# An attention and mixture kernel: the fourth pair's load asked for sooner in the opening, and output by pairs of token blocks on two row tiles with unpadded parts

## The chip, the cores and the metric

The kernel runs on one core of one Trainium2 chip. The metric is the device time of one execution in microseconds (us); lower is better. A core has five engines: TensorE (PE, whose weight loads are listed apart as PEld), VectorE (DVE), ScalarE (ACT), GpSimd (POOL) and SyncE (SP), which in this kernel issues all the DMAs. Each engine works through its own instructions in the order in which the program lists them, and waits on semaphores for the others.

## The reference

Attention over 8 batches and 8 heads, 576 tokens of 64 numbers each, with a decay made of cumulated logarithms of f; then a soft mixture of 8 experts with 4 slots each over all 4,608 tokens. Cut to what matters:

```python
cum = np.cumsum(np.log(np.clip(f, 0.0001, 1.0)), axis=-1)
scores = q @ k.T / 8 + cum[:, None] - cum[None, :]           # causal, per head
attn = softmax(scores) @ v                                    # x: 4608 x 512, heads side by side
logits = x @ phi                                              # 4608 x 32
d = exp(logits - logits.max(0)); d /= d.sum(0) + 1e-09        # over the tokens
slot_input = (d.T @ x).reshape(8, 4, 512)
slot_out[e] = np.maximum(slot_input[e] @ w1[e], 0.0) @ w2[e]  # 512 -> 1024 -> 512
c = exp(logits - logits.max(1)); c /= c.sum(1) + 1e-09        # over the 32 slots
out = c @ slot_out                                            # 4608 x 512
```

The output is 4,608 x 512 numbers of 4 bytes, 9.4 MB. The weights w1 and w2 are 33.6 MB.

## The kernel before, in words

**Attention, by pairs of heads.** There are 32 pairs (`g`, two heads each; head number `i = 2g + h`). `load_qk(g)` brings q and k of a pair, 576 KB, into one of three tiles, `RAW[g % 3]` (line 168). ScalarE rounds them into `WA[g % 3]` and `YA[g % 3]` (`round_k`, `round_q`, lines 177 and 182), DMAs copy the rounded values to the other half of the partitions (`dup_k`, `dup_q`, lines 193 and 197), and GpSimd subtracts them from the raw values, so that `WB` and `YB` hold the low parts (`low_k`, `low_q`, lines 203 and 208). These GpSimd steps are the last readers of a `RAW` tile: a new `load_qk` into it waits for them. TensorE makes the scores once with tokens on the partitions for the row maxima (`s1`, line 224; VectorE takes the maxima in `tops`, line 237; `mturn` and `mrows`, lines 247 to 259, turn them and put them in as a further row of `YA`), and once the other way round for the exponentials (`s2`, lines 274 and 275; `expo` on ScalarE, line 281). GpSimd blanks what lies above the diagonal (`causal`, lines 289 and 292), `s3` (line 309) multiplies by v, `norm` (lines 324 to 329) divides, and `px` (line 336) turns the result. The `s2` products go to a ring of three PSUM banks (`turn`), which `expo` frees; the `s1` products to three others, which `tops` frees.

**The opening.** Lines 496 to 647 are an order written out by hand for the first two pairs, before the loop over `g` from 1 on (line 681). In it SP issues, in this order: the loads of pairs 0 and 1 and the constants, the copies for pair 0, `load_qk(2)` and `load_v(0)` (lines 550 and 551), `dup_k(1)`, `dup_q(1)`, `load_cum(2)` (598 to 600), the row of maxima of head 2 (617), `load_v(1)` and two small constants (618 to 620), `load_qk(3)` (621), the next row of maxima, and the copies for pair 2. `RAW[0]` is the target of `load_qk(3)`; its last reader in the opening is `low_q` of head 1. GpSimd's order there is: `low_k`, `low_q` of heads 0 and 1 (552 to 554), `causal(0)`, `low_k(2)`, `low_q(2)` (608 to 610), `causal(1)`, `low_k(3)`, `low_q(3)` (628 to 630). `first(i, n, busy)` makes the part `n` of the maxima of head `i`, with `busy` matmuls of no use between the scores and the maxima (`warm`, line 489), which keep TensorE at work; `both(i, n)` makes a bank of scores and its exponentials.

**The mixture.** 23 quarters of the weights (512 KB each) have tiles of their own and are loaded during the attention; the other 41 follow into tiles that fall free (`wstream`, line 122). After the last pair come the last logits, the sums over tokens (`dispatch`, line 453), the first layers (`mlp1`, 874; `relu`; `own`, 894) and the second layers (`mlp2`, line 911). `STEPS` sets their order; for experts 4 to 7 the second half of the output's columns is left for the end, lines 997 to 1010.

**The combine weights.** `ctok` holds c for each token; `split(b)` (lines 659 and 660) makes high and low parts of batches b and b + 4 on GpSimd, and `cols(b, ...)` (line 668) turns them, so that `cT` holds, for each token of the first four batches, 128 rows: high and low part of c for a token of the first half (rows 0 to 63) and for the token 2,304 places later (rows 64 to 127).

**The output.** `gathered(n)` (967) sums a half of the 512 columns of the slots' result, `slots(n)` (970) spreads it over the partitions, `halve(h, n)` (976 and 977) makes high and low parts of it for the tokens' half `h`: `SO[h][r]` has values in 64 rows and zeros, set by GpSimd on line 952, in the other 64. `blocks(n0, n1, c)` makes output blocks of 128 tokens: two matmuls over all 128 rows for each (line 992), a copy by ScalarE or VectorE in turn (993) into staging, and one DMA for two blocks (995). The first `FIRST` = 20 blocks of 36 are made in two halves of columns, the others in full width. The staging is six tiles of 1,024 columns, used in turn.

Of the kernel before, what the change touches and what calls it, by code (L numbers as in the profile page):

```python
# [7 lines left out]
F32 = mybir.dt.float32  # L8
# [23 lines left out]
DEFER = 4  # L32
FIRST = 20

# [36 lines left out]
def attn_softmoe(ctx: ExitStack, tc: tile.TileContext, qk, v, f, phi, w1, w2, cst, out):  # L71
# [89 lines left out]
    def turn():  # L161
        ring.append(ring.pop(0))
        return ring[-1]
# [409 lines left out]
    def first(i, n, busy=0):  # L573
        s1(i, *GROUPS[n])
        warm(busy, cs)
        tops(i, *GROUPS[n])
# [6 lines left out]
    for n in range(4):  # L583
        first(0, n, WARM[1])
    first(1, 0, 2 * WARM[1])
    next(r0)
    warm(3 * WARM[1], cs)
    next(r0)
    round_q(1, 0)
    first(1, 1)  # L590
    first(1, 2)
# [4 lines left out]
    round_k(1, 1)  # L596
    round_q(1, 1)
    dup_k(1)
    dup_q(1)
# [20 lines left out]
    nc.sync.dma_start(mk, cst[:, 706:714])  # L620
    load_qk(3)
    round_q(2)
# [31 lines left out]

    def split(b):

        CW[b] = tp.tile([P, NBLK, 2, 2, NS], F32R, name=f"cw{b}", tag="cw", bufs=2)
        hi, lo = (CW[b][:, :, :, r].rearrange("p t h s -> p h t s") for r in range(2))
        nc.gpsimd.tensor_copy(hi, ctok[:, b::4])
        nc.gpsimd.tensor_tensor(lo, ctok[:, b::4], hi.bitcast(F32), op=ALU.subtract)  # L660

# [19 lines left out]
    for g in range(1, NG):  # L681
# [105 lines left out]
        if g == 31:  # L787
            wstream(PTS[:, 0:QW])
            split(0)
            split(1)  # L790
        s3(h1)
# [13 lines left out]
    ring += [ps_s.tile([P, 512], F32, name=f"more{n}", tag="s") for n in range(2)]  # L805
    norm(NH - 1)
    dispatch(b - 1, 0, 1, 2)
    xt(NG - 1, (0, 4), nc.scalar.copy)
# [26 lines left out]
    nc.vector.tensor_scalar_mul(fin[:, 0:2], ones, lrun)  # L835
    split(2)
    dispatch(b, *range(NBLK))
# [81 lines left out]
    for e, k in STEPS[:-4]:  # L919
# [14 lines left out]
        if (e, k) == (3, 0):  # L934
            combine(b, 1)
            combine(b, 2)
            split(3)
        if (e, k) == (0, 6):
            for _ in cols(3, turn):
                pass  # L940
# [18 lines left out]
    pr = [t[:, 0:256] for t in bank]  # L959
    outv = out.rearrange("(n p) c -> p n c", p=P)  # L960
# [10 lines left out]

    def halve(h, *ns):
        rows = slice(64 * h, 64 * h + 64)
        for n in ns:
            c = half[n]
            nc.scalar.copy(SO[h][0][rows, c], pr[n][rows])
            nc.vector.tensor_tensor(SO[h][1][rows, c], pr[n][rows], SO[h][0][rows, c].bitcast(F32), op=ALU.subtract)

    state = [0, 0, 0]

    def blocks(n0, n1, c=slice(0, DM)):

        w = c.stop - c.start
        if state[1] + w * (n1 - n0) > QW:
            state[0:2] = state[0] + 1, 0
        o = stage[state[0] % len(stage)][:, state[1] : state[1] + w * (n1 - n0)]
        state[1] += w * (n1 - n0)
        for n in range(n0, n1):
            h, m = divmod(n, NT // 2)
            pm = turn()[:, 0:w]  # L990
            for r in range(2):
                nc.tensor.matmul(pm, cT[:, 128 * m : 128 * m + 128], SO[h][r][:, c], start=(r == 0), stop=(r == 1))  # L992
            copies[state[2] % 2](o[:, w * (n - n0) : w * (n - n0 + 1)], pm)
            state[2] += 1
        nc.sync.dma_start(outv[:, n0:n1, c], o.rearrange("p (n c) -> p n c", c=w))

# [3 lines left out]
    mlp2(4, 1, 1)  # L1000
    halve(0, 0)
    mlp2(5, 1, 0)
    n = 0
    for e, k in ((5, 1), (6, 0), (6, 1), (7, 0), (7, 1)):
        blocks(n, n + 2, half[0])
        mlp2(e, 1, k)
        blocks(n + 2, n + 3, half[0])
        n += 3
        if n == 9:
            halve(1, 0)  # L1010
    gathered(1)
    blocks(n, n + 2, half[0])
    slots(1)
    blocks(n + 2, n + 3, half[0])
    halve(0, 1)
    blocks(n + 3, FIRST, half[0])
    for n in range(0, FIRST, 2):
        blocks(n, n + 2, half[1])
        if n == 4:
            halve(1, 1)  # L1020
    for n in range(FIRST, NT, 2):
        blocks(n, n + 2)

# [40 lines left out]
```

## Time and profile before

| | |
|---|---|
| time, median of 3 runs | 405.67 us (404.69 to 407.14) |
| the profiled execution's own time | 407.26 us |
| its span, first to last instruction | 405.5 us |
| mean granted TensorE clock | 0.986 |
| busy PE / PEld | 385.3 / 339.3 us |
| busy DVE / ACT / POOL | 281.7 / 259.2 / 257.6 us |
| DMA | 93.72 MB, mean 231 GB/s |

The profile is of one execution, in us from the start of the span. A row of the timeline has the start, the busy time of the rows that were merged, the engine, the line, the operation, the tile written and the tiles read, the shape and the count; in brackets stands how long the engine had been idle before it, and what ended that. A row of a view by windows has, after the window and its length, the busy time of each engine in it with the number of its instructions, the granted clock of TensorE (1.00 is full speed), the mean busy share of the 16 DMA engines, and GB/s.

### The profile page before, as it was taken

The numbers are of one execution on the slowest core, as the hardware profiler recorded it, in microseconds if no ns is written. First come the engines' busy times: TensorE is split into PE (matmuls) and PEld (weight loads), VectorE is DVE, ScalarE is ACT, GpSimd is POOL, SyncE is SP. The second block draws the span as 40 slices with busy tenths as digits, with TensorE's granted clock in tenths as the row PEclk, the third lists the DMA queues.
The fourth block names the chain that finished last, engine by engine and source line by source line (L and its number), as shares of the span: only waits on it lengthen the run. The fifth ranks groups of instructions, "written<-read, shape, count | busy, mean of one in ns | idle before, by whom it ended". The sixth has DMA issues, their size and how long they took to land.

```text
span 405.5 us, 15191 instructions
## 1 busy us (share of the span) xinstructions
PE 385.3 (95%) x5871; PEld 339.3 (84%) x5871; DVE 281.7 (69%) x1127; ACT 259.2 (64%) x660; POOL 257.6 (64%) x351
## 2 busy tenths in 40 slices
PE   7888999999999999999999999999999999899990
PEld 6678999999999999998999999999999885345780
DVE  7784787878787977796879787878787533312571
ACT  8847776767786777686767786778685443100561
POOL 4694788777777777787778777877787742120000
PEclk9996999999999999999999999999999999999997
DMA  6773566677867787768767767777765699999698
GB/s 207 183 183 108 150 174 181 204 205 210 254 192 221 207 238 211 203 191 254 200 197 210 221 205 206 205 207 206 203 172 152 227 360 375 381 408 391 239 368 335
DMA packets 35192, 93.72 MB, mean 231 GB/s; under 512 B 4282, under 2 KB 10096, under 8 KB 35120
## 3 DMA queue, kind: packets, MB, share of 16 engines
q1 hardware_dynamic: 35120, 92.75, 74.0%
q8 instruction: 46, 0.75, 0.8%
q14 instruction: 26, 0.21, 0.1%
HBM read 63.93 MB, written 9.73 MB: 182 GB/s over the span
## 4 chain that ended last, share of the span: by engine, by line
PE 81%; DMA 4%; DVE 3%; ACT 3%; issue 1%; POOL 0%; SPq 0%; DVEq 0%; ACTq 0%
PE pv L309 24%; PE ring L274 13%; PE ring L275 11%; PE s L224 11%; PE pv L336 4%; DMA RAW<-in_qk 3%; PE lg L372 2%; PE pv L911 2%; PE ds L453 2%; PE ring L874 2%; PE pv L874 2%; PE more L992 2%; DVE s L237 1%; DMA out<-RAW 1%; PE ring L911 1%; PE ring L992 1%
## 5 line engine op out<-in xcount | busy, mean ns | idle before, releaser
L281 ACT ACTIVATE PTS<-ring 128x320 f32<-128x320 f32 (+2 forms) x256 | 119.7, 513 | 64.3 <-PE ring L275 36.7
L237 DVE CUSTOM_DVE_ANT_0 s<-s,mask 128x320 f32<-128x320 f32 (+4 forms) x320 | 137.7, 449 | 10.4 <-PE s L224 5.9
L274 PE MATMUL ring<-YA,WA 67*128 67x320 f32 (+9 forms) x384 | 123.3, 334 | 2.7 <-ACT PTS L281 1.7
L275 PE MATMUL ring<-YB,WB 128*128 128x320 f32 (+4 forms) x384 | 111.7, 299 | 0.0
L309 PE MATMUL pv<-V,PTS 128*64 128x65 f32 x3200 | 105.0, 224 | 0.6 <-ACT mr L256 0.6
L309 PEld LDWEIGHTS pv<-V,PTS 128*64 128x64 f32 x3200 | 100.3, 138 | 3.2 <-issue 1.2
L224 PE MATMUL s<-WA,YA 66*128 66x288 f32 (+9 forms) x384 | 98.9, 314 | 1.6 <-ACT YA L182 0.8
L203 POOL TENSOR_TENSOR WB<-RAW,WB 64x576 fp32r<-64x576 f32 x64 | 90.3, 1411 | 11.7 <-DMA WB<-WA 4.9
L208 POOL TENSOR_TENSOR YB<-RAW,YA 64x576 fp32r<-64x576 f32 x64 | 89.3, 1413 | 2.4
L274 PEld LDWEIGHTS ring<-YA,WA 67*128 67x128 f32 (+3 forms) x384 | 70.6, 185 | 9.0 <-issue 2.1
L275 PEld LDWEIGHTS ring<-YB,WB 128*128 128x128 f32 (+1 forms) x384 | 70.8, 184 | 0.0
L224 PEld LDWEIGHTS s<-WA,YA 66*128 66x128 f32 (+1 forms) x384 | 63.6, 192 | 7.3 <-ACT YA L182 1.1
L289 POOL TENSOR_SCALAR_AFFINE_SELECT PTS<-PTS 128x384 f32<-128x384 f32 x64 | 33.3, 521 | 32.0 <-ACT PTS L281 27.8
L292 POOL TENSOR_SCALAR_AFFINE_SELECT PTS<-PTS 128x128 f32<-128x128 f32 (+1 forms) x128 | 31.3, 265 | 34.8 <-ACT PTS L281 32.1
L237 DVE DVE_READ_ACCUMULATOR2_ANT MT<- 128x1 f32 x372 | 52.7, 142 | 0.0
L177 ACT CAST WA<-RAW 64x576 fp32r<-64x576 f32 x64 | 40.0, 669 | 14.2 <-DMA RAW<-in_qk 13.2
L336 PE MATMUL pv<-cs,X 128*128 128x128 f32 x155 | 42.9, 278 | 1.0 <-DVE X L329 0.8
L182 ACT CAST YA<-RAW 64x576 fp32r<-64x576 f32 x64 | 40.0, 670 | 0.4
L237 DVE CUSTOM_DVE_ANT_0 s<-s,mask,MT 128x288 f32<-128x288 f32 x62 | 32.6, 526 | 9.8 <-PE s L224 0.9
L324 DVE TENSOR_SCALAR rl<-pv 128x5 f32<-128x5 f32 x64 | 10.5, 164 | 34.7 <-PE pv L309 33.8
L329 DVE TENSOR_TENSOR X<-pv,rl 128x320 f32<-128x320 f32 (+1 forms) x65 | 31.5, 486 | 2.4 <-DMA YA<-mr 0.3
L360 ACT COPY XT<-pv 128x128 f32<-128x128 f32 (+1 forms) x124 | 28.7, 292 | 0.0
(202 smaller groups left out, 355.1 us busy)
## 6 DMA issues: line engine op xcount, KB each, us to landing
w<-in_w SPq DMA_DIRECT2D x46, 512.0 KB
RAW<-in_qk SPq DMA_DIRECT2D x31, 576.0 KB
V<-in_v SPq DMA_DIRECT2D x32, 325.0 KB
WB<-WA SPq DMA_DIRECT2D x31, 288.0 KB
YB<-YA SPq DMA_DIRECT2D x31, 288.0 KB
p<-in_w SPq DMA_DIRECT2D x7, 512.0 KB
out<-RAW SPq DMA_DIRECT2D x5, 512.0 KB
out<-RAW SPq DMA_DIRECT2D x9, 256.0 KB
```

What stands on the lines that cost most here:

```text
L177: nc.scalar.copy(WA[g % 3][0:64, S * h : S * h + S], RAW[g % 3][64:128, h])
L182: nc.scalar.copy(YA[g % 3][0:64, h, 64:640], RAW[g % 3][0:64, h])
L203: nc.gpsimd.tensor_tensor(t[0:64], RAW[g % 3][64:128, h], t[64:128].bitcast(F32), op=ALU.subtract)
L208: nc.gpsimd.tensor_tensor(YB[g % 2][64:128, h], RAW[g % 3][0:64, h], YA[g % 3][0:64, h, 64:640].bitcast(F32), op=ALU.subtract)
L224: nc.tensor.matmul(t[:, o : o + w], ya[0:m, h, 128 * blk : 128 * blk + 128], wa[0:m, j0 : j0 + w], start=True, stop=True)
L237: nc.vector.tensor_tensor_reduce(out=t[:, o : o + w], in0=t[:, o : o + w], in1=mask[:, m0 : m0 + w], scale=1.0, scalar=top if n == 3 else ...
L274: nc.tensor.matmul(o, wa[0:m, j0 : j0 + n], ya[0:m, h, 64 + i0 : 64 + i0 + w], start=True, stop=False)
L275: nc.tensor.matmul(o, wb[:, j0 : j0 + n], yb[:, h, i0 : i0 + w], start=False, stop=True)
L281: nc.scalar.activation(PT[i % 2][:, SEG_O[bank] : SEG_O[bank] + at], t[:, 0:at], AF.Exp, scale=0.125)
L289: nc.gpsimd.affine_select(d3, d3, pattern=[[0, 3], [1, 128]], compare_op=ALU.is_ge, fill=0.0, base=0, channel_multiplier=-1)
L309: nc.tensor.matmul(o[64 * u : 64 * u + 64, t, :], PT[i % 2][:, at : at + 64], V[:, g % 2, c, 65 * h : 65 * h + 65], start=(c == 0), stop=( ...
L336: nc.tensor.transpose(pm[:, 0:128], x[:, t, 128 * (p % 2) : 128 * (p % 2) + 128], ident)
```

## The change

It has these parts:

1. In the opening, `load_qk(3)` moves from behind `mrows(1, 0, 1)`, `load_v(1)` and two small loads to a place ahead of `dup_k(1)`.
2. In the opening, the second part of the maxima of head 1 is made before the row of maxima of head 0 is turned, with one `warm` matmul after each of the two parts instead of two after the first; two `warm` matmuls instead of three follow.
3. `split` runs on ScalarE (high part) and VectorE (low part) instead of GpSimd; for b = 0 and 1 the two parts are called at different places. `cols(3)` is made after step (1, 6) instead of after step (0, 6).
4. The output is made by pairs: block `m` of the first half of the tokens and block `m` of the second. `SO[r]` has values in all 128 rows; the first block's matmuls read rows 0 to 63, the second's rows 64 to 127, into two PSUM banks. ScalarE copies the one, VectorE the other. The GpSimd zeros go. `FIRST` counts pairs now: the first 8 pairs (16 blocks) are made in two halves of columns. The last `mlp2` calls are no longer interleaved one by one with the blocks, and two PSUM banks join the ring when they fall free.

```diff
-FIRST = 20
+FIRST = 8
...
-    first(1, 0, 2 * WARM[1])
+    first(1, 0, WARM[1])
+    first(1, 1, WARM[1])
     next(r0)
-    warm(3 * WARM[1], cs)
+    warm(2 * WARM[1], cs)
     next(r0)
     round_q(1, 0)
-    first(1, 1)
     first(1, 2)
...
     round_k(1, 1)
     round_q(1, 1)
+    load_qk(3)
     dup_k(1)
     dup_q(1)
...
-    load_qk(3)
     round_q(2)
...
-    def split(b):
+    def split(b, *parts):
...
-        nc.gpsimd.tensor_copy(hi, ctok[:, b::4])
-        nc.gpsimd.tensor_tensor(lo, ctok[:, b::4], hi.bitcast(F32), op=ALU.subtract)
+        if 0 in parts:
+            nc.scalar.copy(hi, ctok[:, b::4])
+        if 1 in parts:
+            nc.vector.tensor_tensor(lo, ctok[:, b::4], hi.bitcast(F32), op=ALU.subtract)
...
-            split(0)
-            split(1)
+            split(0, 0)
+            split(1, 0)
...
     norm(NH - 1)
+    split(0, 1)
+    split(1, 1)
...
-    split(2)
+    split(2, 0, 1)
...
-            split(3)
-        if (e, k) == (0, 6):
+            split(3, 0, 1)
+        if (e, k) == (1, 6):
             for _ in cols(3, turn):
                 pass
...
-            SO = [[sp.tile([P, DM], F32R, name=f"SO{h}{r}") for r in range(2)] for h in range(2)]
-            for h in range(2):
-                for r in range(2):
-                    nc.gpsimd.memset(SO[h][r][64 * (1 - h) : 64 * (1 - h) + 64].bitcast(F32), 0.0)
+            SO = [sp.tile([P, DM], F32R, name=f"SO{r}") for r in range(2)]
...
+    outv = out.rearrange("(h m p) c -> p h m c", h=2, p=P)
...
+    def halve(n):
+        nc.scalar.copy(SO[0][:, half[n]], pr[n])
+        nc.vector.tensor_tensor(SO[1][:, half[n]], pr[n], SO[0][:, half[n]].bitcast(F32), op=ALU.subtract)
...
+        for m in range(m0, m1):
+            pm = [turn()[:, 0:w] for _ in range(2)]
             for r in range(2):
-                nc.tensor.matmul(pm, cT[:, 128 * m : 128 * m + 128], SO[h][r][:, c], start=(r == 0), stop=(r == 1))
-            copies[state[2] % 2](o[:, w * (n - n0) : w * (n - n0 + 1)], pm)
-            state[2] += 1
-        nc.sync.dma_start(outv[:, n0:n1, c], o.rearrange("p (n c) -> p n c", c=w))
+                for h in range(2):
+                    rows = slice(64 * h, 64 * h + 64)
+                    nc.tensor.matmul(pm[h], cT[rows, 128 * m : 128 * m + 128], SO[r][rows, c], start=(r == 0), stop=(r == 1))
+            for h in range(2):
+                copies[h](o[:, h, m - m0], pm[h])
+        if m1 - m0 == 1:
+            nc.sync.dma_start(outv[:, :, m0, c], o[:, :, 0])
+        else:
+            for h in range(2):
+                nc.sync.dma_start(outv[:, h, m0:m1, c], o[:, h])
...
-    halve(0, 0)
-    mlp2(5, 1, 0)
...
+    halve(0)
+    mlp2(5, 1)
+    ring += [bank[0], po[0]]
+    blocks(0, 1, half[0])
+    blocks(1, 2, half[0])
+    mlp2(6, 1)
+    blocks(2, 3, half[0])
+    blocks(3, 4, half[0])
+    mlp2(7, 1)
     gathered(1)
-    blocks(n, n + 2, half[0])
+    blocks(4, 6, half[0])
     slots(1)
...
+    blocks(6, FIRST, half[0])
+    halve(1)
+    ring += [bank[1], po[1]]
+    for m in range(0, FIRST, 2):
+        blocks(m, m + 2, half[1])
+    for m in range(FIRST, NT // 2):
+        blocks(m, m + 1)
```

More of the change, by code (lines that the diff above doesn't have):

```diff
@@ L653, in attn_softmoe @@
     CW = {}
-    def split(b):
-        CW[b] = tp.tile([P, NBLK, 2, 2, NS], F32R, name=f"cw{b}", tag="cw", bufs=2)
+    def split(b, *parts):
+        if 0 in parts:
+            CW[b] = tp.tile([P, NBLK, 2, 2, NS], F32R, name=f"cw{b}", tag="cw", bufs=2)
         hi, lo = (CW[b][:, :, :, r].rearrange("p t h s -> p h t s") for r in range(2))
-        nc.gpsimd.tensor_copy(hi, ctok[:, b::4])
-        nc.gpsimd.tensor_tensor(lo, ctok[:, b::4], hi.bitcast(F32), op=ALU.subtract)
+        if 0 in parts:
+            nc.scalar.copy(hi, ctok[:, b::4])
+        if 1 in parts:
+            nc.vector.tensor_tensor(lo, ctok[:, b::4], hi.bitcast(F32), op=ALU.subtract)
     def cols(b, bank):
@@ L959, in attn_softmoe @@
     pr = [t[:, 0:256] for t in bank]
-    outv = out.rearrange("(n p) c -> p n c", p=P)
     NT = B * S // P
+    outv = out.rearrange("(h m p) c -> p h m c", h=2, p=P)
     stage = [t.rearrange("p a b -> p (a b)") for t in RAW] + p2 + p0
@@ L970, in slots, with blocks @@
         nc.tensor.matmul(pr[n], srep, so[:, half[n]], start=True, stop=True)
[L972 to L977, printed above, removed]
+    def halve(n):
+        nc.scalar.copy(SO[0][:, half[n]], pr[n])
+        nc.vector.tensor_tensor(SO[1][:, half[n]], pr[n], SO[0][:, half[n]].bitcast(F32), op=ALU.subtract)
     state = [0, 0, 0]
-    def blocks(n0, n1, c=slice(0, DM)):
+    def blocks(m0, m1, c=slice(0, DM)):
         w = c.stop - c.start
-        if state[1] + w * (n1 - n0) > QW:
+        n = 2 * w * (m1 - m0)
+        if state[1] + n > QW:
             state[0:2] = state[0] + 1, 0
[L986 to L990, printed above, removed]
-            for r in range(2):
-                nc.tensor.matmul(pm, cT[:, 128 * m : 128 * m + 128], SO[h][r][:, c], start=(r == 0), stop=(r == 1))
-            copies[state[2] % 2](o[:, w * (n - n0) : w * (n - n0 + 1)], pm)
-            state[2] += 1
-        nc.sync.dma_start(outv[:, n0:n1, c], o.rearrange("p (n c) -> p n c", c=w))
+        o = stage[state[0] % len(stage)][:, state[1] : state[1] + n].rearrange("p (h m c) -> p h m c", h=2, c=w)
+        state[1] += n
+        for m in range(m0, m1):
+            pm = [turn()[:, 0:w] for _ in range(2)]
+            for r in range(2):
+                for h in range(2):
[8 more added lines that the diff above has]
+                nc.sync.dma_start(outv[:, h, m0:m1, c], o[:, h])
     gathered(0)
@@ L1000, in attn_softmoe @@
     mlp2(4, 1, 1)
-    halve(0, 0)
-    mlp2(5, 1, 0)
-    n = 0
-    for e, k in ((5, 1), (6, 0), (6, 1), (7, 0), (7, 1)):
-        blocks(n, n + 2, half[0])
[L1006 to L1010, printed above, removed]
+    halve(0)
[7 more added lines that the diff above has]
+    mlp2(7, 1)
     gathered(1)
-    blocks(n, n + 2, half[0])
+    blocks(4, 6, half[0])
     slots(1)
[L1014 to L1022, printed above, removed]
+    blocks(6, FIRST, half[0])
[5 more added lines that the diff above has]
+        blocks(m, m + 1)
 def kernel(q, k, v, f, moe_phi, moe_w1, moe_w2):
```

## The prediction

> **What bounds the kernel now.** I read the page first, then the chain of waits, then windows and the timeline of the two stages that the change touches: the opening, and the output.
>
> ```profile
> span 405.5 us, 15191 instructions
> ...
> PEclk9996999999999999999999999999999999999997
> ...
> RAW<-in_qk SPq DMA_DIRECT2D x31, 576.0 KB
> ```
>
> TensorE has full clock in every slice but the fourth (30 to 40 us) and the last, when its work is done. So the fourth is looked at first: by windows the second pair (g = 1) and the third, and two single microseconds of the second.
>
> ```profile
> 26.98:41.79 14.81, 12.36 (x144) 11.32 (x143) 8.69 (x35) 9.49 (x21) 8.85 (x12) 0.77 0.53 138
> 41.79:50.67 8.88, 8.88 (x145) 8.49 (x143) 7.25 (x30) 6.76 (x17) 6.91 (x11) 1.00 0.49 143
> 30.00:31.00 1.00, 0.11 (x1) 0.00 (x0) 0.97 (x6) 0.98 (x3) 0.00 (x0) 1.00 0.85 205
> 33.00:34.00 1.00, 1.00 (x6) 0.81 (x4) 0.94 (x4) 0.60 (x1) 0.13 (x2) 0.50 0.08 32
> ```
>
> The same 144 matmuls take 14.81 us in one pair and 8.88 in the next, where TensorE never idles: 5.93 us too many. They are idle time (0.11 us busy in the first of the two microseconds) and half clock thereafter (0.50 in the second). Picked rows of the timeline, with the others between them left out, say why TensorE idles.
>
> ```profile
> 13.86 1.42 POOL L208 TENSOR_TENSOR YB<-RAW,YA 64x576 fp32r<-64x576 f32 x1
> ...
> 17.09 0.48 SPq L193 DMA_DIRECT2D WB<-WA  x1
> 20.38 1.41 POOL L203 TENSOR_TENSOR WB<-RAW,WB 64x576 fp32r<-64x576 f32 x1 [1.57 <-PE ring L275]
> 23.56 0.37 SPq L168 DMA_DIRECT2D RAW<-in_qk  x1
> 23.82 0.49 POOL L292 TENSOR_SCALAR_AFFINE_SELECT PTS<-PTS 128x128 f32<-128x128 f32 x2
> 24.61 0.92 PE L309 MATMUL pv<-V,PTS 128*64 128x65 f32 x24 [0.26 <-ACT mr L256]
> 28.78 1.24 ACT L177 CAST WA<-RAW 64x576 fp32r<-64x576 f32 x2 [4.22 <-DMA RAW<-in_qk]
> 29.01 0.33 PE L336 MATMUL pv<-cs,X 128*128 128x128 f32 x1 [0.78 <-DVE X L329]
> 31.78 0.39 PE L274 MATMUL ring<-YA,WA 67*128 67x256 f32 x1 [1.67 <-ACT PTS L281]
> ```
>
> The fourth pair's load is issued at 23.56 and ScalarE stands 4.22 us until it has landed. Its four casts then lie ahead of the exponentials that free the PSUM ring, and TensorE stands 1.67 us at 31.78. The gap of 0.78 us before it is VectorE's (the first `norm`s), and isn't the load's. `RAW[0]`, the target, had its last reader done at 13.86 + 1.42 = 15.28: the load could have gone 8.3 us sooner.
>
> In the last stage the weights stream first, then the output. Here are four rows of its timeline, the first a stall of TensorE before `cols(3)`, and its windows.
>
> ```profile
> 352.52 0.44 PE L668 MATMUL lg<-cs,cw 128*128 128x128 f32 x2 [1.36 <-POOL cw L660]
> ...
> 374.83 3.84 SPq L995 DMA_DIRECT2D out<-RAW  x6
> 381.48 0.59 PE L970 MATMUL ring<-so,cs 128*128 128x256 f32 x2
> 383.15 0.38 PE L992 MATMUL ring<-SO,cT 128*128 128x256 f32 x1 [0.23 <-DVE SO L977]
> ```
>
> ```profile
> 350.00:355.00 5.00, 3.64 (x33) 1.23 (x29) 0.92 (x4) 0.86 (x3) 1.56 (x3) 1.00 1.03 413
> 375.00:380.00 5.00, 4.93 (x46) 3.06 (x44) 2.46 (x6) 2.59 (x7) 0.00 (x0) 1.00 0.74 256
> 380.00:385.00 5.00, 4.77 (x40) 4.00 (x38) 3.37 (x9) 2.63 (x9) 0.00 (x0) 1.00 0.62 212
> 385.00:390.00 5.00, 4.98 (x33) 4.32 (x32) 3.73 (x10) 3.44 (x9) 0.00 (x0) 1.00 1.02 342
> 395.00:400.00 5.00, 1.32 (x6) 0.75 (x4) 1.58 (x3) 1.17 (x2) 0.00 (x0) 1.00 1.05 399
> ```
>
> From 385 on the DMA engines are full (share 1.02 and more) and TensorE ends long before them: the end is output bandwidth. From 375 to 385 they are not (0.74, 0.62), while TensorE is nearly full: there TensorE, with blocks and `mlp2` interleaved, feeds them too slowly, and the second half of the columns can't begin before `slots(1)` at 381.48 and its `halve` at 383.15.
>
> **The change part by part.** The sum is made against the profiled execution: 407.26 us, its span of 405.5 and 1.76 around it. That is 1.59 above the median of 405.67.
>
> *The load.* In its new place SP comes to it behind `load_v(0)` and waits until 15.28; `dup_k(1)`, behind it on SP, is held by ScalarE until 17.09 anyway, so SP's queue loses nothing. The DMA queue may.
>
> ```profile
> 16.00:16.50 0.50, 0.50 (x7) 0.50 (x5) 0.47 (x5) 0.47 (x3) 0.00 (x0) 1.00 1.03 406
> 17.50:18.00 0.50, 0.50 (x4) 0.30 (x2) 0.43 (x2) 0.50 (x2) 0.00 (x0) 1.00 0.00 0
> ```
>
> 576 KB (590,000 bytes) at 406 GB/s are 1.45 us. The engines are full before 17.5, then empty for half a microsecond; the load would move from about 17.4 to 18.9, ahead of `dup_k(1)`. Of the 1.45 us the hole takes about half, so that `dup_k(1)` lands about 0.9 us later (bounds 0 and 1.45). GpSimd's 1.57 us of idleness before 20.38 is the wait for that copy (the matmul named had no part in it), and behind it stand `low_q(2)`, `causal(1)` (ending 23.82 + 0.49 = 24.31) and then `s3(1)` on TensorE at 24.61. That has 0.3 us of slack. So the early load costs TensorE about 0.7 us at 24.61 (0 to 1.15), and VectorE's `norm` behind it as much.
>
> What it gains: the casts run right after the row of maxima at about 24.6 to 27, the exponentials of the second pair no longer wait, and the gap of 1.67 us goes. Late next is VectorE's gap of 0.78, which stays. Half clock began less than a microsecond after the gap; I take it to be the gap's effect, since it is the only one of that size before the output's end: the 1.36 us at 352.52 had no such effect (clock 1.00 in that window).
>
> Without both, pair g = 1 takes what its neighbour takes: 5.93 - 0.78 (gap that stays) - 0.7 (late start) = 4.45 us gained; I take 4.3, since VectorE comes out of its crowded stretch a little behind. Bounds: 5.15 without any delay of `dup_k`; 1.67 - 0.7 = 0.97 if the half clock stays. Behind this stage TensorE is full until the weights' stream, so what is gained here is passed on whole.
>
> The Trainium skill (TensorE: Matmul & The Clock Gate, Part 1) puts the fall to half clock down to an idle window of about 3.4 us, and asks for gaps under some 3 us. Going by that, a gap of 1.67 us would not have done it, and the half clock would have another cause; the trace, with its fall right behind this gap, speaks for a shorter measure.
>
> *The reordered `warm` matmuls.* One is left out, and the second maxima move into a time in which VectorE idles 1.31 us:
>
> ```profile
> 14.39 0.47 DVE L237 CUSTOM_DVE_ANT_0 s<-s,mask 128x288 f32<-128x288 f32 x1 [1.31 <-PE s L224]
> ```
>
> What follows hangs on ScalarE, whose first exponentials start when the first scores are there, at best one `warm` matmul sooner. That is a few tenths, inside the bounds left open above, and nothing if the added score matmul takes its place; it stays out of the sum.
>
> *`split`.* GpSimd's two steps before `cols(3)` become a ScalarE cast and a VectorE subtraction, and `cols(3)` moves behind more `mlp2` work: the 1.36 us at 352.52 go. That is no gain at the end by itself, since the weights' stream fills the DMA there (1.03), but TensorE comes to the last `mlp2` 1.36 us sooner. The parts for b = 0 and 1 cost VectorE about 2 x 0.49 us (as its 128x320 product), ahead of a copy before which it idles 1.37 us; without that cover they would push the last logits back by 1.0.
>
> ```profile
> 28.46 0.49 DVE L329 TENSOR_TENSOR X<-pv,rl 128x320 f32<-128x320 f32 x1
> 334.20 0.42 DVE L345 COPY XT<-ring 128x256 f32<-128x256 f32 x1 [1.37 <-PE ring L336]
> ```
>
> *The output.* The DMA's shortage from 375 to 385 is 5 x (342 - 256) + 5 x (342 - 212) = 1,080 KB, at 342 GB/s 3.2 us. Further, 16 blocks instead of 20 go out in pieces of 1 KB: four blocks, 1.05 MB, at 399 instead of 342, 0.44 us. Ceiling: 3.6.
>
> ```profile
> 374.53 0.43 PE more L992 x2
> 374.96 0.23 PE lg L992 x2
> ```
>
> ```profile
> L993 DVE COPY p<-more 128x256 f32<-128x256 f32 x5 | 2.1, 424 | 0.9 <-PE more L992 0.7
> L993 DVE COPY RAW<-more 128x512 f32<-128x512 f32 x3 | 2.1, 692 | 1.0 <-PE more L992 1.0
> L992 PE MATMUL more<-SO,cT 128*128 128x512 f32 x16 | 4.4, 395 | 0.0
> ```
>
> A block costs TensorE 0.23 us, and 0.20 more behind an `mlp2`; a pair on two row tiles 0.23 if they run beside each other, 0.46 if not; its two copies 0.42, side by side; its 256 KB of DMA 0.77. So either way the DMA is the slowest, once the order lets blocks through. Before `slots(1)` stood 17 blocks (3.9 us of TensorE), and now stand six pairs (1.4 us overlapped, 2.8 not), with TensorE 1.36 sooner: from 381.48 it comes to 377.6 to 379.0. I take 378, and the second half's blocks 1.7 behind it as before (383.15 - 381.48), at 379.7 instead of 383.15. In the meantime eight pairs (2.1 MB) are there for 375 to 380, which can take 1.7. What is left is a gap or two of half a microsecond, where the next DMA waits for a copy. I take 2.3 of the 3.6; bounds 0.5 (blocks late for another reason) and 3.6.
>
> Sum: 407.26 - 4.3 - 2.3 = 400.7.
>
> **The rivals.** *The half clock stays* (its cause is not the gap): 407.26 - 0.97 - 2.3 = 404.0, within half a per cent of the median, about what a measurement can tell from no change. Against it: nowhere else in 400 us does the clock fall while there is work.
>
> *The early load costs what it brings.* Before, 28.78 - 23.56 = 5.2 us went by from its issue to its landing. If it holds `dup_k(1)` till 22.8 instead of 20.38, `s3(1)` starts 2.2 us later, a gap as long as the one removed, with its half clock; the second pair's start is lost about as much as the gap brings, within 0.5: 407.26 + 0.5 - 2.3 = 405.5. It decides from a delay of about 2 us on. Against it: 406 GB/s just before.
>
> *The row tiles don't overlap, nor hide their loads* (slower). Then each matmul costs what a lone one does, 0.38 us at 256 columns and 0.395 at 512. From 379.7 on there are 8 pairs x 4 x 0.38 and 10 pairs x 4 x 0.395, 28.0 us, to 407.7, then the last copy, 0.69, and the last DMA, 4.47 by the chain's row:
>
> ```profile
> 392.14 4.47 DMA out<-RAW
> ```
>
> That is 412.9 against 405.5, 7.4 later; with the opening's 4.3, 407.26 + 7.4 - 4.3 = 410.4. It decides from where a pair costs more than its 0.77 us of DMA, 0.19 a matmul. Against it: 0.115 a matmul now, two in 0.23.
> The Trainium skill (TensorEngine Tiling (Array Packing), Key Properties) says that a change of the tiling mode, though not of the tile alone, drains TensorE, and that tiles take in and multiply in parallel; so it is for this rival only where blocks and `mlp2` alternate, which the change does less often. The 0.20 us more behind an `mlp2` agrees with a drain at a change of mode; no row of before shows two row tiles.
>
> **How the numbers follow.** The forecast has 0.76, the half clock 0.09, the costly load 0.08, the row tiles 0.07. The predicted time is 400.7. The low end is both upper bounds, 407.26 - 5.15 - 3.6 = 398.5; the high end takes in the half clock's 404.0 with a little less from the output, 404.4; outside lie the last two cases and a little of the first. Faster by over half a per cent (below 403.6) is the first case, 0.76; within it the next two, 0.17; slower the last, 0.07.
>
> **What would show it.** Right: the load issued about 15.3, no wait of ScalarE for it, clock 1.00 from 30 to 40 us, the third pair starting about 37.5 instead of 41.79; `low_k(2)` on GpSimd about 21.3; no wait before `cols(3)`; the DMA share near 1 from 376 on (in the new time some 4 us sooner), pairs at 0.23. Wrong: clock 0.50 behind another gap; GpSimd's idle time before 20.38 grown by over 2 us; TensorE full until the last output DMA.

## The result, and the profile after

| | before | after |
|---|---|---|
| median of 20 runs each, side by side | 406.67 us (403.45 to 410.59) | 401.93 us (399.99 to 438.54) |
| the profiled execution: time, span | 407.26, 405.5 us | 404.26, 402.5 us |
| its mean granted clock | 0.986 | 0.971 |

The ratio is 0.989, with a 95% interval of 0.986 to 0.991. The median lies in the forecast's range, 398.5 to 404.4 us, and 1.2 above its point of 400.7. The gain is further off: the sum takes 6.6 us from an execution of 407.26 us, and the medians differ by 4.7. The profile shows why: the half clock, whose removal was half of the forecast's gain (3.3 us: 4.3 with it, 0.97 without), is still there. Two lines of the page after:

```profile
span 402.5 us, 15135 instructions
...
PEclk9959999999999999999999999999999999999985
```

The weak slice was the fourth (30 to 40 us), and is now the third (20 to 30). The windows of after show it at its edges. The third pair starts at 40.17 us in its timeline, where 41.79 was before and 37.5 was forecast. Columns as in the prediction: busy time of PE, PEld, DVE, ACT and POOL, then the clock, DMA share and GB/s.

```profile
17.24:20.65 3.41, 2.01 (x14) 1.53 (x12) 2.66 (x11) 3.36 (x8) 0.49 (x2) 1.00 0.99 295
20.65:24.06 3.41, 3.41 (x34) 3.19 (x35) 2.29 (x12) 2.45 (x6) 2.71 (x2) 0.50 0.45 112
24.06:27.48 3.42, 3.27 (x42) 2.80 (x40) 0.92 (x6) 0.64 (x2) 3.20 (x6) 0.50 0.18 55
27.48:30.89 3.41, 3.41 (x51) 3.06 (x48) 2.06 (x10) 2.10 (x4) 3.40 (x3) 0.50 0.50 97
30.89:34.30 3.41, 3.41 (x31) 3.04 (x27) 3.12 (x15) 1.64 (x5) 0.52 (x1) 1.00 0.96 266
```

Three windows of 3.41 us are at half clock, one more than before (32.64 to 39.47), and they follow one in which TensorE was idle 3.41 - 2.01 = 1.40 us. Each costs up to half its length, 1.7 us. The timeline of after says what that idle time was, and that the load did what was expected of it:

```profile
15.46 0.33 SPq L168 DMA_DIRECT2D RAW<-in_qk  x1
...
18.93 0.47 PE L274 MATMUL ring<-YA,WA 98*128 98x448 f32 x1 [1.40 <-ACT YA L568]
...
21.29 1.40 POOL L203 TENSOR_TENSOR WB<-RAW,WB 64x576 fp32r<-64x576 f32 x1 [2.62 <-DMA WB<-WA]
...
27.09 1.24 ACT L177 CAST WA<-RAW 64x576 fp32r<-64x576 f32 x2
```

The load is issued at 15.46 (15.3 forecast), ScalarE's casts no longer wait for it, and GpSimd's `low_k(2)` starts at 21.29 (21.3 forecast) instead of 20.38. But at 17.5 to 18.9 TensorE waits for a row of maxima (line 568, `next(r1)`). Before had this wait too, shorter, and the prediction doesn't mention it:

```profile
19.06 0.47 PE L274 MATMUL ring<-YA,WA 98*128 98x448 f32 x1 [1.05 <-ACT YA L568]
```

Executions of one kernel differ, among other things, by how many such windows they get; the ratios leave out the few that were much disturbed (the medians and ranges hold all), and where single executions are named, the mean clock of each tells them apart: one window at half clock in 402 us takes 3.41 x 0.5 / 402 = 0.004 from it.

In the output stage the timeline of after has these rows:

```profile
352.10 0.44 PE L671 MATMUL lg<-cs,cw 128*128 128x128 f32 x2
...
371.52 0.38 PE L993 MATMUL ring<-SO,cT 64*128 64x256 f32 x1
371.52 0.38 PE L993 MATMUL more<-SO,cT 64*128 64x256 f32 x1
371.75 0.27 PE L993 MATMUL ring<-SO,cT 64*128 64x256 f32 x1
...
373.72 0.64 PE L916 MATMUL pv<-w,X 128*32 128x256 f32 x8 [0.89 <-DMA w<-in_w]
...
376.25 0.64 PE L916 MATMUL pv<-w,X 128*32 128x256 f32 x8 [0.63 <-DMA w<-in_w]
...
377.47 0.70 PE L972 MATMUL ring<-so,cs 128*128 128x256 f32 x2
...
379.61 0.38 PE L993 MATMUL pv<-SO,cT 64*128 64x256 f32 x1 [0.78 <-ACT SO L975]
```

`cols(3)` no longer waits. The two row tiles start together (371.52 both), and both their second matmuls follow 0.23 us later. `slots(1)` stands at 377.47 (378 forecast, 381.48 before), the second half's first block at 379.61 (379.7 forecast). What wasn't forecast is that TensorE, with less to do, now waits for the weights of the last `mlp2` steps, 0.89 and 0.63 us. The windows of after:

```profile
375.00:380.00 5.00, 3.59 (x38) 1.83 (x36) 2.95 (x8) 2.04 (x7) 0.00 (x0) 1.00 0.64 218
380.00:385.00 5.00, 4.93 (x54) 4.75 (x55) 4.06 (x12) 3.98 (x11) 0.00 (x0) 1.00 1.00 350
```

The DMA is full from 380 on, five microseconds sooner than before (212 GB/s in that window then, 350 now). From 375 to 380 it still isn't (0.64), where I had expected it near 1 from 376.

### The profile page after: what moved, and what is told of

Read it like the earlier page. It is cut to its first block, busy times and chain, and to the rows that moved or that the text cites. A ratio compares the mean times of both kernels' runs of the same rounds, so it can differ in the third digit from the quotient of the medians.

```text
span 402.5 us, 15135 instructions
## 1 busy us (share of the span) xinstructions
PE 379.9 (94%) x5861; PEld 333.7 (83%) x5861; DVE 281.3 (70%) x1127; ACT 258.6 (64%) x660; POOL 251.0 (62%) x339
## 4 chain that ended last, share of the span: by engine, by line
PE 81%; DMA 8%; ACT 2%; DVE 1%; issue 1%; ACTq 0%; DVEq 0%; SPq 0%
PE pv L309 25%; PE ring L274 14%; PE ring L275 12%; PE s L224 12%; DMA w<-in_w 5%; PE pv L336 4%; PE lg L372 3%; PE ds L453 2%; PE pv L879 1%; DMA out<-p 1%; PE pv L916 1%; DMA YA<-mr 1%; DMA out<-RAW 1%; PE pv L247 1%; PE ring L879 1%; PE tk L436 1%
## 5 line engine op out<-in xcount | busy, mean ns | idle before, releaser
L309 PE MATMUL pv<-V,PTS 128*64 128x65 f32 x3200 | 106.9, 226 | 0.5 <-ACT mr L256 0.3
L309 PEld LDWEIGHTS pv<-V,PTS 128*64 128x64 f32 x3200 | 102.1, 140 | 3.4 <-issue 1.4
```

The lines of the kernel that those rows point to most:

```text
L309: nc.tensor.matmul(o[64 * u : 64 * u + 64, t, :], PT[i % 2][:, at : at + 64], V[:, g % 2, c, 65 * h : 65 * h + 65], start=(c == 0), stop=( ...
```

## The experiments

**One part at a time.** Three kernels have one part of the change each; a fourth fills, in the kernel before, the gap of 1.67 us with TensorE work of no use.

The load alone:

```diff
+    load_qk(3)
     dup_k(1)
...
-    load_qk(3)
     round_q(2)
```

> The kernel before with nothing changed but the place of the fourth pair's load, ahead of the second pair's copies. Gap theory (half clock comes when TensorE idles more than about 1.4 us within one window of 3.4 us, and each such window costs TensorE about half of it): the gap of 1.67 us at 30 to 32 us goes, the one at 18 us stays at about 1.0, which did not bring the clock down before; clock 1.00 all through the opening in most executions, second pair (from its first score matmul to the third pair's) about 9.3 instead of 14.8 us, time 3.0 to 4.5 us shorter than before. Stall theory (the half clock belongs to the opening and only its place is accidental): half clock stays somewhere before 45 us, and the time is 1 us shorter. Either way the copy of the second pair lands 0.9 us later, so that GpSimd starts on it at about 21.3 instead of 20.4.

Measured: 403.68 us, ratio 0.993 (0.989 to 0.996). Seven of its 12 executions have clocks of 0.990 to 0.995 (401.82 to 404.78 us); none of the 35 of before that ran beside it is above 0.989 (of the 46 of before that ran beside the later kernels, eight are at 0.990 to 0.992). In the execution that was profiled, `low_k(2)` starts at 21.57, TensorE has no gap above 0.78 us between 20 and 33, the clock is full there from 22.79 on, and the third pair starts at 38.12. So the gap at 31 us and its half clock did go. There is one window at half clock, and it is at another place:

```profile
15.96:19.37 3.41, 2.27 (x18) 1.80 (x17) 3.08 (x14) 3.31 (x8) 1.22 (x6) 1.00 0.98 350
19.37:22.79 3.42, 3.42 (x17) 3.23 (x15) 1.84 (x9) 3.13 (x8) 1.22 (x1) 0.50 0.58 130
```

It follows the old gap of 1.05 us at 18, which in before's profile had no such effect.

The reordered `warm` matmuls alone:

```diff
-    first(1, 0, 2 * WARM[1])
+    first(1, 0, WARM[1])
+    first(1, 1, WARM[1])
     next(r0)
-    warm(3 * WARM[1], cs)
+    warm(2 * WARM[1], cs)
     next(r0)
     round_q(1, 0)
-    first(1, 1)
```

> The kernel before with nothing changed but the order of the second head's maxima and the useless matmuls in the opening (one left out, the second maxima ahead of the turning of the first row). Gap theory: TensorE runs ahead by 0.4 us and then waits for the same ScalarE copy, so the gap at 18 us grows from 1.0 to 1.4 us, half clock comes at about 20 us in a good part of the executions and the gap at 30 us brings it as well in others; time 0 to 2 us longer than before, clock lower. If the reordering is the small gain it looks like on the timeline (ScalarE's chain 0.15 us sooner): 0.1 to 0.2 us shorter, not to be told from the kernel before.

Measured: 404.44 us, ratio 0.996 (0.992 to 0.999). No execution was longer than before's median by more than 0.2 us, and the gain of 2.2 us by medians is more than the 0.1 to 0.2 of the other theory, so both expectations failed. Its timeline shows what this part does to the two gaps of TensorE:

```profile
18.93 0.47 PE L274 MATMUL ring<-YA,WA 98*128 98x448 f32 x1 [1.40 <-ACT YA L568]
...
32.44 0.58 PE L274 MATMUL ring<-YA,WA 67*128 67x256 f32 x1 [2.47 <-ACT PTS L281]
```

The gap at 18 us is 1.40, as in after. In the three other kernels of this group, which have the old order, it is 1.05 or 1.06. So it is the reorder that lengthens it: the second maxima's matmuls used to lie behind the copy of the first row and now lie ahead of it, and TensorE comes to the second row's wait that much sooner. And yet no half clock follows here; the windows give a likely reason:

```profile
17.82:21.24 3.42, 2.31 (x16) 2.05 (x16) 2.79 (x12) 3.35 (x9) 1.48 (x3) 1.00 0.90 182
21.24:24.65 3.41, 3.16 (x66) 2.73 (x66) 2.32 (x13) 2.13 (x5) 3.19 (x6) 1.00 0.47 123
28.06:31.48 3.42, 1.13 (x8) 0.86 (x7) 2.60 (x11) 2.02 (x4) 1.78 (x2) 1.00 0.95 214
31.48:34.89 3.41, 2.45 (x11) 2.36 (x12) 0.55 (x1) 2.13 (x7) 0.52 (x1) 0.50 0.48 182
```

An edge of the 3.41 us grid falls at 17.82, inside the gap of 17.53 to 18.93: of its 1.40 us, 0.29 lie in one window and 1.11 in the next. In after the whole gap lay in one. (The 1.11 us alone are no proof: 1.06 and 1.14 us in one window had half clock behind them in two of the other kernels.) The 2.29 us of idleness in the window from 28.06 were followed by half clock.

Everything but the opening (the new output and `split`, the opening of before):

> The opening of the kernel before with all the rest of the change (split on ScalarE and VectorE, cols(3) later, output by pairs on row tiles). If the output part is worth what the prediction took: 2.3 us shorter than before, with the half clock at 32 to 39 us still there. If the tail is bound by the DMA engine that is last with the weights, and not by the blocks: under 1 us.

Measured: 406.45 us, ratio 1.000 (0.996 to 1.004): no gain that can be measured, against both expectations. Its profile has the new output working, but a gap of 2.95 us at 30 and three windows at half clock behind it (31.61 to 41.85), where before had two. Its third pair starts at 43.97 us, 2.2 later than in before's profile, while from the first `mlp1` to the end of the span it takes 62.40 us against 64.26. In this execution, then, the opening lost what the end gained (1.9). So this run doesn't weigh the output by itself; the next group does.

Useless matmuls in before's gap at 30 to 32:

```diff
         px(g - 1, 1)
+        if g == 1:
+            fill_pe(9, 0)   # 9 matmuls of 59 columns on constants
         s2(h0, 3)
```

> The kernel before with nine useless matmuls of 59 columns put into the gap at 30 to 32 us (they read constants and write 59 unused columns of a PSUM bank; the output is as before). The wait of ScalarE for the load and the late exponentials stay, so the scores after the gap start no sooner. Gap theory: clock 1.00 through the opening, 2.5 to 3.5 us shorter than before. Stall theory: the same time as before or a little longer.

Measured: 404.82 us, ratio 0.996 (0.993 to 1.000). Seven of 12 executions have clocks of 0.990 to 0.995 and take 402.61 to 405.04 us; five, at 0.981 to 0.985, take 405.30 to 406.87. By medians that is 1.85 us shorter than before, under the 2.5 to 3.5 of the gap theory; the seven alone have a median of 403.31, which is 3.4 shorter. Nothing was sped up; TensorE was only kept busy. The profile is one of the five:

```profile
17.38:20.79 3.41, 2.35 (x16) 1.81 (x14) 2.79 (x13) 3.36 (x8) 0.89 (x3) 1.00 0.76 152
20.79:24.20 3.41, 3.41 (x34) 3.19 (x35) 2.30 (x12) 2.46 (x6) 3.28 (x5) 0.50 0.44 114
```

Again it is the gap at 18 us, 1.06 long, here with three windows behind it.

**The gap at 18 us filled too.** Four kernels get matmuls of the same kind ahead of the waiting step:

```diff
     round_k(2)
+    fill_pe(6, 1)   # 4 in the other three
     both(1, 0)
```

The changed kernel with it:

> The changed kernel with six useless matmuls of 59 columns (about 0.21 us each, 1.2 us in all) into TensorE's gap at about 18 us; the output is unchanged. Gap theory (the short idle of TensorE at 18 us sets the half clock of the changed kernel's opening, in part of the executions, and the move of the load only took away the one at 30 us): no window at half clock before the end of the mixture in any execution, granted clock about 0.985 (only the output's last microseconds at half clock), 400.5 us in most executions, where the changed kernel goes from 400.0 to 405.6. Rival (the half clock belongs to the load of the opening itself, and not to the gap): half clock between 20 and 31 us as before, 402 us and clocks from 0.971 to 0.985.

Measured: 400.82 us (400.40 to 402.19), ratio 0.987 (0.982 to 0.991); all six clocks from 0.979 to 0.986. The profile has no window at half clock before 385, with TensorE's work nearly done, and the third pair starts at 37.73:

```profile
16.00:20.00 4.00, 3.95 (x33) 3.62 (x32) 3.03 (x14) 3.90 (x8) 1.36 (x7) 1.00 0.98 336
20.00:25.00 5.00, 4.74 (x83) 4.14 (x80) 3.88 (x19) 3.91 (x10) 2.81 (x3) 1.00 0.60 158
...
37.73 0.47 PE L274 MATMUL ring<-YA,WA 67*128 67x448 f32 x1
```

By these clocks the changed kernel itself had a clean opening in 8 of 18 executions (0.981 to 0.985, 399.99 to 401.70 us); in the others it was 0.971 to 0.978, up to 405.55.

The kernel before with the load moved and the gap filled, and the changed kernel with the old `warm` order and the gap filled, differ by the output and `split` alone:

> The kernel before with the load moved and four useless matmuls of 59 columns in the gap at 18 us: the opening should be free of half clock in all executions, with before's output. Gap theory: granted clock 0.990 to 0.995, 402.3 us (the better executions of the load alone gave 401.8). Rival (the half clock comes from elsewhere): 403.7 us, as with the load alone.

> The changed kernel with the old order of the useless matmuls and four more in the gap at 18 us: the same opening as the kernel before with the load moved and its gap filled, with the changed output and split. If the output is worth what the forecast gave it (2.3): 400.0 us. If it is worth what the profiles of the parts run so far show between the last weight's landing and the end (about 1.3): 401.0 us. If the output part is worth nothing, as its run alone had it: 402.3 us.

Measured: 403.67 us (ratio 0.992, 0.988 to 0.997) and 401.46 us (0.987, 0.981 to 0.993). With a clean opening, which 8 executions of the first (0.993 to 0.996) and 5 of the second (0.983 to 0.987) had, the medians are 402.60 and 400.63: output and `split` together are worth 2.0 us (1.8 by means), between the two expectations. Eight and five executions are few: they spread from 401.31 to 403.91 and from 400.22 to 401.66. The traces agree. The stretch from the first `mlp1` to the end of the span takes 63.4 to 64.3 us in the five kernels with before's output, and 62.0 to 62.5 in the six with after's: 1.7 less in the mean.

"All executions clean" failed: the first kernel's median over all executions is the rival's number (403.7), and both profiles fell into the rest. They are long executions (409.36 and 406.84 us), so they show what can happen here, not what is usual. For the second, GpSimd and TensorE in the timeline:

```profile
23.59 1.40 POOL L203 TENSOR_TENSOR WB<-RAW,WB 64x576 fp32r<-64x576 f32 x1 [4.74 <-DMA WB<-WA]
...
27.32 0.65 PE L309 MATMUL pv<-V,PTS 128*64 128x65 f32 x10 [1.99 <-POOL PTS L292]
```

`low_k(2)` starts at 23.59 and not at 21.3: the load ahead of `dup_k(1)` held that copy 3.2 us, not 0.9. TensorE idles 1.99 us for it at 27.32, and half clock follows from 29.02 to 39.26. The other kernel's profile has the same start (23.38) and a smaller gap, 0.97 at 27.12; its windows are

```profile
23.20:26.61 3.41, 1.88 (x34) 1.42 (x29) 1.71 (x10) 1.50 (x4) 3.10 (x3) 1.00 0.43 117
26.61:30.02 3.41, 2.90 (x33) 2.55 (x35) 1.33 (x6) 1.31 (x3) 3.27 (x5) 0.50 0.75 145
```

No single gap was long there: one of 0.81 us, one of 0.26 and the first 0.46 of the 0.97 add up to 1.5 in the window.

The last of the four has the parts of the slots' result padded with zeros again, so that there are no row tiles, but keeps the order by pairs:

```diff
-        nc.scalar.copy(SO[0][:, half[n]], pr[n])
-        nc.vector.tensor_tensor(SO[1][:, half[n]], pr[n], SO[0][:, half[n]]...)
+        for h in range(2):   # 64 rows each, into SO[h][r]
+            nc.scalar.copy(SO[h][0][rows, c], pr[n][rows])
+            nc.vector.tensor_tensor(SO[h][1][rows, c], pr[n][rows], SO[h][0][rows, c]...)
...
-                    nc.tensor.matmul(pm[h], cT[rows, ...], SO[r][rows, c], ...)
+                    nc.tensor.matmul(pm[h], cT[:, ...], SO[h][r][:, c], ...)
```

> The one before, with the parts of the slots' result padded with zeros to 128 rows again, so that each block's two matmuls use all rows and pairs no longer lie on two row tiles; the order by pairs stays. If the DMA bounds the output: the same within 0.3 us, a pair's four matmuls at 0.46 us beside 0.64 us or more of DMA. If TensorE's rate does: 18 pairs with 26 groups of four matmuls, 0.23 us more for each group that lies on the path, up to 6 us.

Measured: 402.28 us, ratio 0.990 (0.986 to 0.993); its nine executions with clocks of 0.991 to 0.994 have a median of 401.85, which is 1.2 above the 400.63 of the one before it. So "the same within 0.3" failed: the padding and the lone row tile cost more than half of what the output brings (in its trace, with 63.94 us from the first `mlp1` on, all of it). The trace has two candidates: twice the TensorE time for a pair, and longer `halve` steps, here for the second half of the columns, where the unpadded kernel waits once, for 0.78 us:

```profile
377.39 0.39 PE L1003 MATMUL pv<-SO,cT 128*128 128x256 f32 x1 [0.61 <-ACT SO L986]
378.25 0.39 PE L1003 MATMUL ring<-SO,cT 128*128 128x256 f32 x1 [0.46 <-ACT SO L986]
```

**Rate or parts, the load's place, and the clock by itself.** The next four are made from the changed kernel with its gap filled (400.82 us). They did not run beside it: the kernel before, which ran beside both groups, had medians of 407.50 us then and 407.11 now. So a difference of a microsecond between the groups is not shown by the times alone.

Every output matmul made twice, so that a pair takes TensorE what it would without row tiles:

```diff
-            for r in range(2):
+            for r in (0, 1, 0, 1):
```

> The changed kernel with the gap at 18 us filled and every output matmul made twice (the first time to no use; the output is unchanged): a pair of 256 columns takes TensorE 0.46 us, as without row tiles, and one of 512 columns 0.93; the parts of the slots' result stay unpadded and are made by two instructions. If the 1.2 us that the padding cost are TensorE's rate: 402.0 us. If they are the longer making of the parts: 400.8.

Measured: 403.47 us, ratio 0.994 (0.990 to 0.998). The eight executions with clocks from 0.990 on have a median of 402.9, 2.1 above, and its trace takes 63.60 us from the first `mlp1` on, where the filled kernel's takes 62.27. The other four, at 0.972 to 0.988, had more half clock than these, though this opening is the filled one; where it lay in them, no trace tells.

The parts of the slots' result made by two copies and two subtractions of 64 rows, the row tiles kept:

```diff
-        nc.scalar.copy(SO[0][:, half[n]], pr[n])
-        nc.vector.tensor_tensor(SO[1][:, half[n]], ...)
+        for h in range(2):   # 64 rows each
+            nc.scalar.copy(SO[0][rows, c], pr[n][rows])
+            nc.vector.tensor_tensor(SO[1][rows, c], ...)
```

> The changed kernel with the gap at 18 us filled and each half of the parts of the slots' result made by two copies and two subtractions of 64 rows, as with the padding, instead of one of each on 128 rows; the row tiles stay. If the 1.2 us that the padding cost are the making of the parts (about 0.8 us more for the second half of the columns): 401.6 to 402.0 us. If they are TensorE's rate: 400.8.

Measured: 405.25 us, ratio 0.996 (0.992 to 1.000); the shortest two 401.38 and 402.01. Each theory had one of the two kernels at 400.8, and both came out longer. From the first `mlp1` on, the trace takes 63.79 us here, 63.60 with the matmuls doubled and 63.94 with the padding: either change alone goes with nearly as much as both, and they don't add up. How much of the 63.79 the making of the parts costs by itself isn't separated, for this trace also has half clock in the stretch. Its windows show that: TensorE's two waits at the second `halve`, 0.76 and 0.47 us, are most of 1.30 us of idle time in one window, and half clock follows, now in the middle of the output.

```profile
374.49:377.91 3.42, 2.12 (x16) 1.19 (x15) 2.19 (x6) 1.79 (x7) 0.00 (x0) 1.00 0.55 187
377.91:381.32 3.41, 3.41 (x31) 3.41 (x33) 2.86 (x7) 2.63 (x8) 0.00 (x0) 0.50 0.87 305
```

That is one execution, at 0.981; those of 404 us and more have clocks of 0.979 and lower, which goes with their being the longest, and where their further windows at half clock lie isn't known.

The load behind both copies instead of ahead of them:

```diff
-    load_qk(3)
     dup_k(1)
     dup_q(1)
+    load_qk(3)
```

> The changed kernel with the gap at 18 us filled, and the load of the fourth pair issued behind both copies of pair 1 instead of ahead of them. If the load's 1.45 us of DMA ahead of the copy of k cost what the forecast says (0.9 us at GpSimd, 0.7 at TensorE): 400.1 us, against 400.8 with the load ahead, with the second product of the opening no longer waiting about 0.65 us for GpSimd's blanked scores. If VectorE sets that stretch anyway: 400.8.

Measured: 399.84 us (399.62 to 400.39), ratio 0.984 (0.980 to 0.989), the lowest time of all and the narrowest. It is 1.0 below the filled kernel's 400.82 by medians that were not taken side by side, and the intervals of the two ratios (0.982 to 0.991 there) overlap. The traces show 0.57: the third pair starts at 37.16 instead of 37.73, GpSimd waits as long as before the change, and the 0.65 us are gone:

```profile
20.24 1.41 POOL L203 TENSOR_TENSOR WB<-RAW,WB 64x576 fp32r<-64x576 f32 x1 [1.57 <-PE ring L275]
...
37.16 0.47 PE L274 MATMUL ring<-YA,WA 67*128 67x448 f32 x1
```

Last, the disputed rule by itself: stalls of TensorE put into the attention, where it is otherwise full.

```diff
+    def stall(n):
+        fill_pe(1, 0)
+        nc.scalar.copy(gs[:, 0:59], pv[0][:, 453:512])
+        for _ in range(n):
+            nc.scalar.copy(gs, cs[:, 0:128])
+        nc.tensor.matmul(pv[0][:, 453:512], cs[:, 0:128], gs[:, 0:59], start=True, stop=True)
...
         tops(u1, 0, 1)
+        if g in STALL:
+            stall(STALL[g])
         s2(h1, 3, 4)
```

> The changed kernel with the gap at 18 us filled and 14 stalls put into every second pair from the fourth to the thirtieth: TensorE waits for one small ScalarE copy of its own product, and for 0 to 7 more behind it, so that it idles some 0.6 to 2.2 us each time where it is otherwise full; the output is unchanged. Gap theory: half clock behind the longer stalls, none behind stalls of under 1 us, each time for one window of 3.41 us or a few; with the sum of the idle time in one window of TensorE's clock record as the measure, nearly always from 1.4 us on, and sometimes between 1.05 and 1.4. Rival (the half clock belongs to the opening and its small matmuls): no window at half clock in these pairs. Time 415 to 450 us, which isn't the point.

Measured: 461.35 us in the one execution, above the 450 expected: the stalls came out longer than planned, with up to 2.92 us of idle time in a window. Ten of the 14 were followed by half clock. Some of the windows, on the grid of the clock's own record, the first of them from the opening:

```profile
24.14:27.55 3.41, 1.62 (x27) 1.33 (x27) 1.27 (x6) 2.74 (x5) 3.19 (x6) 1.00 0.40 83
...
75.34:78.75 3.41, 2.35 (x36) 2.14 (x38) 1.90 (x8) 1.40 (x5) 1.38 (x2) 1.00 0.09 32
78.75:82.16 3.41, 3.41 (x70) 3.41 (x67) 1.22 (x8) 3.22 (x8) 3.10 (x4) 0.50 0.75 148
82.16:85.57 3.41, 3.41 (x42) 2.98 (x39) 1.95 (x8) 1.18 (x4) 1.57 (x2) 1.00 0.87 240
...
119.71:123.12 3.41, 2.62 (x19) 2.13 (x18) 3.20 (x15) 2.39 (x9) 2.27 (x5) 1.00 0.64 236
123.12:126.54 3.42, 2.44 (x52) 2.37 (x54) 1.14 (x8) 1.88 (x5) 0.66 (x3) 1.00 0.01 2
126.54:129.95 3.41, 3.41 (x78) 3.00 (x75) 1.70 (x6) 3.34 (x9) 3.25 (x4) 1.00 0.79 156
...
143.60:147.01 3.41, 1.35 (x9) 0.92 (x8) 2.19 (x11) 2.76 (x11) 2.29 (x4) 1.00 0.32 128
147.01:150.43 3.42, 3.35 (x30) 3.25 (x32) 1.12 (x5) 0.96 (x4) 0.30 (x2) 0.50 0.03 7
150.43:153.84 3.41, 3.41 (x67) 3.41 (x67) 1.72 (x7) 2.34 (x4) 3.25 (x4) 0.50 0.88 173
```

A window with 3.41 - 2.35 = 1.06 us of idle time is followed by one at half clock, one with 2.06 by two. A stall of 0.79 + 0.98 = 1.77 us (two gaps around the first of its matmuls), parted by an edge of the grid at 123.12, has none behind it. From 7 us on, where the trace's clock record begins, all 12 windows with 1.05 us or more are followed by half clock, and none of the 14 with 0.41 to 0.98. The rival, that this belongs to the opening, is out. One of the 12 is the first window above: in the filled opening itself, `low_k(2)` started at 22.94, TensorE waited 1.54 us for blanked scores at 26.69, and two windows at half clock followed. So filling the gap at 18 us doesn't keep this opening clean when the early load holds the copy for long.

## Why the prediction was right, and where it wasn't

*The gap and its half clock.* Right in its cause: with the gap at 31 us gone, by the load (b_load) or by useless work (b_fill), the clock behind it stays full. The size was right too, where the opening is clean: the third pair starts at 37.73 in the filled kernel, 4.1 us sooner than before, against 4.3. In after as it stands the profile has 1.6 of it (40.17). What failed is the reason by which I took the gap for the only danger, "since it is the only one of that size". There was another of 1.05 us at 18, and the measure, as far as these traces go and with the exceptions named at the end, is not the length of a gap but the idle time inside one window of a grid of 3.41 us. From about 1.05 us on, half clock followed in every window of the stalled kernel. The grid does not start with the kernel (17.24, 17.82 and 15.96 are edges in three runs of nearly the same opening), so that the same gap is split in some executions and not in others. That is one source of the spread from run to run: after's 399.99 to 405.55 us became 400.40 to 402.19 with the gap filled. It is not the only one, for eight executions with clocks of 0.993 to 0.996 (the kernel before with load and filled gap) still differ by 2.6 us. The Trainium skill (TensorE: Matmul & The Clock Gate, Part 1) gives such a free-running window, of 3413 ns, and these edges agree; its rule, no idle gaps above about 3.4 us, does not reach down to the 1.06 us that were enough here.

*The reordered `warm` matmuls.* "A few tenths, inside the bounds" left out a cost: they lengthen the gap at 18 us from 1.05 to 1.40. Whole inside a window, that is enough: after's profile pays three windows for it. Its time, 404.26 us, is that of the rival "the half clock stays" (404.0), by another road. Of the 18 executions 8 have the clean opening that the forecast counted on (median 401.21 us); the other 10 have a median of 403.2. That the median of all lies as near to 400.7 as it does is partly luck: it depends on how many executions the grid spares. That the reorder alone came out shorter than before by 2.2 us of median isn't explained; its profile shows no gain in the opening (third pair at 42.04).

*The early load's cost.* 0.9 us at GpSimd fits the profiled execution (21.29 against 20.38), but that was luck. In the nine traces with the load ahead of the copies, `low_k(2)` starts at 21.29 to 23.59, the middle one at 22.14; 21.29 is the least, and seven of the nine are later than the prediction's upper bound (20.38 + 1.45 = 21.83). (The working's "about half" is half a microsecond taken from 1.45, and 0.9 less 0.3 of slack is 0.6, not 0.7.) Why the copy can come later than the load's own 1.45 us would make it, the runs don't show. At TensorE the cost is smaller, 0.57 us at the third pair's start (37.73 against 37.16). The rival "the early load costs what it brings", with its point at 2 us, did occur in single executions (23.59). Placed behind the two copies the load doesn't delay GpSimd and is still in time.

*`split`.* The stall ahead of `cols(3)` is gone. What this part is worth by itself no run shows: it was always measured together with the output.

*The output.* The row tiles overlap, as forecast; `slots(1)` and the second half come where the sum put them. The term came out at 2.0 by clean executions (1.7 by the traces) instead of 2.3. Mis-sized is what the DMA gets from 375 to 380: 218 GB/s x 5 us = 1.1 MB instead of 1.7. In that stretch TensorE waits 0.63 us for weights that come by the same DMA and 0.78 for `halve`, and just before it 0.89 for weights; the next blocks stand behind these waits. And one sentence of the working fell: "either way the DMA is the slowest" (0.23 or 0.46 us for a pair against 0.77). Doubling the output matmuls costs about 2 us (1.4 in the traces). A likely reason, argued and not shown by itself, is that at the start of each half there is nothing in store: the DMA waits for the first blocks, so TensorE's rate and the time of `halve` count there, though the DMA bounds the stage as a whole. The windows from 375 to 380 fit that: 292 GB/s in the filled kernel, 264 with the matmuls doubled, 245 with the padding, 218 with the parts made in two (which has half clock there).

*Left open:* why the output with before's opening showed no gain (b_tail). In the one execution with a trace the opening was 2.2 us worse than before's, but that all 12 should lose some 2 us by it was not shown, nor why it should be worse with the same code.

## What to carry to other kernels

Add up TensorE's idle time over any 3.41 us, and don't look at the longest gap alone: here windows with about 1.05 us or more cost, in most cases, one to four windows at half clock. Four to nine useless matmuls in the gap, in time that was idle anyway, kept them away in many executions, though not in all. A transfer that is asked for sooner is better put behind the short copies that someone waits for than ahead of them. And where the DMA bounds a stage on the whole, look at the places where its queue is empty: there the producer's rate may be the price.

## What was not expected of the hardware

- Half clock in the middle of full work, behind windows with 1.05 to 1.07 us of idle time. But 1.05 is not a fixed limit: in the openings of the other kernels, windows of 1.05 to 1.14 had it behind them in two executions and not in three. The window of 1.36 us ahead of `cols(3)` (350 us, before) had none, while in the output on two row tiles 0.79 us (385.88 to 389.29, after) and 0.81 us (382.34 to 385.75, the filled kernel) had it. Which work a window holds may count too, and no run here tells.
- Its length is whole windows, one to four (26.61 to 40.27). What sets the number is open: behind 1.72 us of idle time there were three (29.02 to 39.26), though TensorE never idled in them, and behind 1.70 us (170.91 to 174.32, with the stalls) one.
- The same 288 KB copy behind the same 576 KB load reached GpSimd between 0.9 and 3.2 us late in nine traces.
